# A recurrent attention with a token and channel mixer: the same operations in another issue order and other buffers

## The chip, the cores and the metric

The kernel runs on one core of one Trainium2 chip. The metric is the time of one execution on the device in microseconds (us); less is better. The core has a matrix engine (TensorE, PE in the profile, with PEld for its weight loads), three engines that work through elements (VectorE or DVE, ScalarE or ACT, GpSimd or POOL), SyncE (SP), which here only issues transfers, and 16 DMA engines that carry them.

## The reference

Four batches, eight heads, 768 steps, 48 values a head. A gated linear attention runs along the steps with a state of 48 x 48 a head; its output, heads side by side, is the input of a mixer over tokens and then over channels.

```python
for t in range(S):
    state = alpha[:, :, t, :, None] * state + np.einsum('bhd,bhe->bhde', k[:, :, t], v[:, :, t])
    y[:, :, t] = np.einsum('bhd,bhde->bhe', q[:, :, t], state)
...
xt = x.transpose(0, 2, 1)
h = np.maximum(xt @ w_tok1, 0.0) @ w_tok2
u = x + h.transpose(0, 2, 1)
h2 = np.maximum(u @ w_ch1, 0.0) @ w_ch2
return (u + h2).astype(np.float32)
```

## The kernel before

**Attention** is computed in 12 blocks n = 0 to 11, three to a batch, 256 steps each. Four loads bring alpha, k, q and v of a block (`ld_at`, `ld_kt`, `ld_qt`, `ld_vt`, 384 KB each). ACT takes the logarithm of alpha (`ln`; from block 3 on first the product of two neighbouring steps, `P`, on DVE or POOL, then `lnP`), PE sums it along the steps (`cum`), ACT takes the exponential of the sum and of its negative (`E`, `IE`), and DVE or POOL scales q and k with them (`qq`, `kk`). k and q are then turned: in blocks 0 to 5 by PE (`trk`, `trq`) with a copy out of PSUM (`evk`, `evq`), in blocks 6 to 11 by a DMA transpose (`dk`, `dq`, with a copy `pq`). PE multiplies the two (`G0`, `G1`, one for each half of the block), DVE masks the product (`mask0`, `mask1`), and PE multiplies it with v (`y0`, `y1`) on top of what the state gives (`ia`, `ib`). v is cast and shifted between halves (`vb`, `vs0`, `vs1`), k likewise (`ka`, `kb`, `kc`); `K` is the block's share of the state, `sa` adds the state so far and `sm` scales the sum. `x0`, `x1` take the result out of PSUM.

**The mixer** runs once a batch b: `t1_b_m_kc` multiplies the six pieces of x with the first token weights, `ht` is the ReLU, `t2_b_i` the second token matmul, `u_b_i` adds x. u is turned by PE (`up`, `ut`, batch 0) or a DMA transpose (`ux_b_half`, batches 1 to 3). `c1_b_mc_half` is the first channel matmul in 24 pieces of three instructions, `rt` its ReLU, `c2_b_i_q` the second in quarters of three instructions, `o_b_i` adds u and `st_b_i` stores the tile. The last tile of the last batch is cut into two halves of 192 columns (`h0`, `h1`). Weights are loaded in pieces of 384 KB (`ldw_wt..`, `ldw_wc..`) and cast (`cw_..`) on ACT, DVE or POOL.

**The order is written out as a list.** `build` lists all operations with what each needs; `ORDER` is one list of all their names, and the last letter of each says the engine: t for PE, s for ACT, v for DVE, g for POOL, y for SyncE. The kernel emits them in that order, so on each engine they run in the order in which they stand in the list, and an operation that waits holds all behind it on its engine. `BUFS` gives the number of the buffer for each value in the order in which the values first appear. A value that takes a number used before waits until the readers of the earlier one are done. The pools matter for this: 19 input buffers of 384 KB for all loads (class `in`), 20 buffers for `rt`, 3 for `o`, and eight PSUM banks, in which every PE result lies (class `one` takes one, `pair` two).

**Fillers.** Names such as `f8_trk0` are matmuls on zeros that write nothing that is used. The number counts units of 512 columns; three units are done as one float32 matmul, which the profile shows as two records, the rest as bfloat16 matmuls:

```python
for _ in range(count // 3):
    ...
    self.mm(self.bank(bank)[0:64, 0:384], w, m, True, True)
for _ in range(count % 3):
    ...
    self.mm(self.bank(bank), z, m, True, True)
```

In the profile most attention matmuls and the fillers stand at line 643, the turning by PE at 712, t1 at 878, t2 at 883, c1 at 902, c2 at 907; loads at 584, weight loads at 600 to 607, stores at 624, DMA transposes at 725 and 729. Copies and casts are at 745 (ACT) and 746 (DVE, POOL), the masks at 770, `u` at 887, `o` at 911, `rt` and `ht` at 873 (ACT) and 875 (DVE).

Of the kernel before, what the change touches and what calls it, by code (L numbers as in the profile page):

```python
# [424 lines left out]
ld_kt4y qq4g s0_3v ln15s G1_3t sa1_3v c1_0_2_1t rt_0_2_1s mask0_3v lnP5s c1_0_1_0t c1_0_5_1t rt_0_5_1s rt_0_1_0s r15s
mask1_3v ldw_wc21y cw_wc21s k0a4g ldw_wc20y c1_0_6_1t rt_0_6_1v c1_0_4_0t kk4v ldw_wc22y c1_0_5_0t c1_0_0_0t cw_wc22s
rt_0_4_0v rt_0_0_0v cw_wc20g rt_0_4_1s c1_0_6_0t rt_0_6_0v c1_0_3_1t trq4t rt_0_3_1v cum5t trk4t ld_kt5y k0a5g
ldw_wc23y rt_0_5_0s c2_0_3_0t c2_0_5_0t evq4s kb4s evk4v ld_qt5y G1_4t mask1_4v G0_4t ld_vt4y c2_0_0_0t IE5s c2_0_0_1t
ka4g cw_wc23s c2_0_3_1t kc4s sm1_3g E5s mask0_4v ib3t y1_3t ldw_wc24y cw_wc24s c2_0_5_1t vb4g vs1_4s x1_3s ia4t
ldw_wc25y vs0_4g cw_wc25s ld_at6y y0_3t kk5v c2_0_3_2t y0_4t q0r5v trk5t evk5s qq5v K4t c2_0_0_2t sa0_4v c2_0_0_3t P6v  # L430
x0_3s ld_at7y sm0_4g o_0_0v trq5t x0_4s sa1_4v P7g evq5s lnP6s c2_0_5_2t c2_0_5_3t ld_vt5y vb5g c2_0_4_0t c2_0_4_1t
ld_kt7y kc5g G1_5t G0_5t lnP7s o_0_5v ib4t y1_4t vs1_5s mask1_5v t1_1_1_0t t1_1_1_1t sm1_4g x1_4s c2_0_4_2t c2_0_3_3t
vs0_5s ld_at8y t1_1_1_2t st_0_5s K5t mask0_5v sa0_5v sm0_5v cum6t t1_1_0_0t ld_kt6y k0a6g t1_1_0_1t ld_qt6y c2_0_2_0t
ln17s ld_qt7y ia5t y0_5t x0_5s IE6s kk6g ib5t y1_5t ln16s E6s t1_1_0_2t x1_5v t1_1_0_3t t1_1_1_3t cum7t E7s o_0_3v
# [531 lines left out]
```

## Time and profile before

| What | Value |
|---|---|
| Runs of the kernel | 161.95, 162.28, 163.87 us; median 162.28 |
| Span of the profiled execution, first to last instruction | 160.5 us |
| PE busy | 154.6 us, 96% of the span, 1563 matmul records |
| DVE, ACT, POOL busy | 114.9, 97.8, 80.8 us (72, 61, 50%) |
| Moved by DMA | 35.05 MB, mean 218 GB/s |
| Instructions | 3971 |

For the profiled execution only the span is on record. Times below are counted from the span's start. A row of the timeline gives start, length, engine, line, operation, what is written and read, the shapes, and in brackets how long the engine was idle before and what ended that. A row of the groups gives the number of instructions, their busy time, the mean duration of one in ns, and the idle time ahead of them. A row of stretches gives busy time and number of instructions of each engine, the granted PE clock, the share of the DMA engines and GB/s.

### The profile page before, as it was taken

The numbers are of one execution on the slowest core, as the hardware profiler recorded it, in microseconds if no ns is written. First come the engines' busy times: TensorE is split into PE (matmuls) and PEld (weight loads), VectorE is DVE, ScalarE is ACT, GpSimd is POOL, SyncE is SP. The second block draws the span as 40 slices with busy tenths as digits, with TensorE's granted clock in tenths as the row PEclk, the third lists the DMA queues.
The fourth block names the chain that finished last, engine by engine and source line by source line (L and its number), as shares of the span: only waits on it lengthen the run. The fifth ranks groups of instructions, "written<-read, shape, count | busy, mean of one in ns | idle before, by whom it ended". The sixth has DMA issues, their size and how long they took to land.

```text
span 160.5 us, 3971 instructions
## 1 busy us (share of the span) xinstructions
PE 154.6 (96%) x1563; PEld 97.1 (60%) x1563; DVE 114.9 (72%) x206; ACT 97.8 (61%) x179; POOL 80.8 (50%) x94
## 2 busy tenths in 40 slices
...
DMA packets 76130, 35.05 MB, mean 218 GB/s; under 512 B 70352, under 2 KB 74320, under 8 KB 76112
## 3 DMA queue, kind: packets, MB, share of 16 engines
q1 hardware_dynamic: 73808, 31.76, 74.1%
...
q8 instruction: 12, 0.20, 0.5%
...
HBM read 25.17 MB, written 4.72 MB: 186 GB/s over the span
## 4 chain that ended last, share of the span: by engine, by line
PE 61%; DMA 12%; DVE 6%; ACT 6%; SPq 6%; POOL 4%; issue 3%; DVEq 0%; POOLq 0%
PE ps L907 22%; PE ps L902 21%; PE ps L643 11%; DMA in<-in_v_dram 6%; SPq L584 6%; DMA out_dram<-o 4%; PE ps L878 3%; PE ps L883 2%; DMA ut<-u 2%; DVE pkk L700 2%; DVE gtm L770 1%; PE ps L712 1%; DVE rt L875 1%; POOL vb L746 1%; POOL pkq L700 1%
## 5 line engine op out<-in xcount | busy, mean ns | idle before, releaser
L907 PE MATMUL ps<-wc,rt 128*128 128x384 bf16 (+1 forms) x300 | 52.4, 319 | 0.0
L902 PE MATMUL ps<-ut,wc 128*128 128x384 bf16 x288 | 50.3, 326 | 0.1
L902 PEld LDWEIGHTS <-wc 128*128 128x128 bf16 x288 | 27.1, 98 | 17.9 <-DMA ut<-u 0.6
L907 PEld LDWEIGHTS <-rt 128*128 128x128 bf16 x300 | 27.8, 98 | 16.0
L873 ACT ACTIVATE rt<-ps 128x384 bf16<-128x384 f32 x47 | 21.4, 492 | 23.6 <-PE ps L902 23.3
L875 DVE TENSOR_SCALAR rt<-ps 128x384 bf16<-128x384 f32 x49 | 25.6, 551 | 9.1 <-PE ps L902 8.9
L770 DVE TENSOR_TENSOR gtm<-ps,mk 128x1024 bf16<-128x1024 f32 x24 | 28.5, 1218 | 3.1 <-PE ps L643 2.8
L911 DVE TENSOR_TENSOR o<-ps,u 128x384 f32<-128x384 f32 (+1 forms) x25 | 13.2, 536 | 12.6 <-PE ps L907 10.1
L700 POOL TENSOR_TENSOR pkk<-in,IE 128x768 bf16<-128x768 f32 x8 | 14.5, 1817 | 3.3 <-DVE ss L844 2.3
L745 ACT CAST x<-ps 128x384 bf16<-128x384 f32 x20 | 9.2, 479 | 11.1 <-PE ps L643 9.5
L887 DVE TENSOR_TENSOR u<-ps,x 128x384 bf16<-128x384 f32 x24 | 12.0, 550 | 3.1 <-PE ps L883 2.5
L746 POOL CAST vb<-in 64x384 bf16<-64x384 f32 (+1 forms) x14 | 8.3, 594 | 10.4 <-DMA in<-in_v_dram 4.7
L692 POOL TENSOR_TENSOR in<-in,in 128x384 f32<-128x384 f32 x8 | 8.0, 1000 | 10.5 <-DVE u L887 3.8
L643 PE MATMUL ps<-rt 128*128 128x512 bf16 (+1 forms) x29 | 12.1, 515 | 1.1 <-DVE rt L541 1.1
L745 ACT CAST vb<-in 64x384 bf16<-64x384 f32 (+1 forms) x18 | 11.4, 634 | 0.8 <-DMA in<-in_v_dram 0.3
L700 POOL TENSOR_TENSOR pkq<-in,E 128x768 bf16<-128x768 f32 x6 | 10.9, 1818 | 0.6 <-DMA tpk<-pkq 0.3
L878 PE MATMUL ps<-x,wt 128*128 128x384 bf16 x48 | 11.0, 325 | 0.0
L844 POOL TENSOR_TENSOR ss<-tmp,E 128x384 bf16<-128x384 f32 x10 | 8.3, 833 | 4.2 <-DVE in L628 3.9
L841 DVE TENSOR_TENSOR tmp<-ps,ss 128x384 f32<-128x384 f32 x16 | 8.8, 552 | 1.8 <-PE ps L643 0.6
L883 PE MATMUL ps<-ht,wt 128*128 128x384 bf16 x48 | 9.1, 326 | 0.0
L643 PE MATMUL ps<-vb,gtm 128*128 128x48 bf16 x192 | 8.2, 183 | 0.2 <-DVE gtm L770 0.2
L643 PE MATMUL ps<-tpq,tpk 48*64 48x128 bf16 (+1 forms) x288 | 7.9, 218 | 0.4 <-POOL tpq L746 0.3
...
## 6 DMA issues: line engine op xcount, KB each, us to landing
in<-in_alpha_dram SPq DMA_DIRECT2D x12, 384.0 KB, 5.1
in<-in_v_dram SPq DMA_DIRECT2D x12, 384.0 KB, 5.6
in<-in_k_dram SPq DMA_DIRECT2D x12, 384.0 KB, 5.2
in<-in_q_dram SPq DMA_DIRECT2D x12, 384.0 KB, 5.5
in<-in_moe_w_ch_dram SPq DMA_DIRECT2D x12, 384.0 KB, 5.9
...
in<-in_moe_w_tok_dram SPq DMA_DIRECT2D x4, 384.0 KB, 6.0
...
```

The source lines that it names most:

```text
L643: return self.pe.matmul(out, lhsT=lhsT, rhs=rhs, start=start, stop=stop, skip_group_check=True)
L700: self.shared(self.eng[e].tensor_tensor(self.t(dst)[:, :, h0:h1, 0:D], self.t(src)[:, h0:h1].rearrange("p h s d -> p s h d"), bass.AP(tens ...
L745: return self.act.copy(d, s)
L770: self.nc.vector.tensor_tensor(self.t(gtm)[:, hf, :, :], self.pair(gp).rearrange("p a (j t) -> p (a j) t", t=128), bass.AP(tensor=m.tensor ...
L873: self.act.activation(d, s, AF.Relu)
L875: self.nc.vector.tensor_scalar_max(d, s, 0.0)
L878: self.pe.matmul(self.bank(bank)[:, 0:HD], lhsT=self.wt1[:, kc, m * 128 : m * 128 + 128], rhs=self.t(x), start=(kc == 0), stop=(kc == NS - 1))
L883: self.pe.matmul(self.bank(bank)[:, 0:HD], lhsT=self.wt2[:, kc, i * 128 : i * 128 + 128], rhs=self.t(hts[kc]), start=(kc == 0), stop=(kc = ...
L887: self.nc.vector.tensor_tensor(self.t(u)[:, i % 3], self.bank(bank)[:, 0:HD], self.t(x), ALU.add)
L902: self.pe.matmul(self.bank(bank)[:, 0:HD], lhsT=self.wc1[:, kc, mc * 128 : mc * 128 + 128], rhs=self.t(ut)[:, 3 * half : 3 * half + 3, kc, ...
L907: self.pe.matmul(self.bank(bank)[:, 0 : cz - ca], lhsT=self.t(rts[mc][0])[:, i * 128 : i * 128 + 128], rhs=self.wc2[:, mc, ca:cz], start=( ...
L911: self.nc.vector.tensor_tensor(self.t(o)[:, ca:cz], self.bank(bank)[:, 0 : cz - ca], self.t(u)[:, i % 3, ca:cz], ALU.add)
```

## The change

`ORDER` and `BUFS` are replaced by others; nothing else is touched. The change describes itself as issue order and buffer numbers searched from the present ones with instruction fetches counted on one DMA engine, every operation left as it was. Between the two lists only fillers differ in kind and number (13 entries with 36 units before, 9 with 25 after). Of the other operations some move to another engine: on POOL 79 entries in place of 82, on DVE 186 for 183, on ACT 192 for 194, on SyncE 93 for 91 (two more stores go out from there). The diff, cut to the start and the end of the order and the first line of the buffers:

```diff
-ld_at1y ld_at0y ln1s ln0s f8_cumw1t f1_cumw1t cumw1t IE1s cumw0t IE0s ld_vt0y E0s vb0g vs0_0g vs1_0v ld_kt0y kk0v
-f8_trk0t f1_trk0t trk0t E1s ld_qt0y qq0v ka0s kb0s kc0v f1_trq0t trq0t ld_kt1y kk1v K0t evq0s s0_0v ld_vt1y vb1s
-f1_trk1t trk1t ld_at2y evk0v ln2s f2_G0_0t G0_0t ld_qt1y ka1g sa1_0v f4_cumw2t cumw2t mask0_0v vs0_1s kb1g kc1g vs1_1s
-K1t sm1_0g qq1v sa0_1v sm0_1v G1_0t ld_kt2y IE2s E2s trq1t evq1s ib0t mask1_0v f3_y1_0t y1_0t y0_0t evk1v G0_1t sa1_1v
-ld_qt2y x1_0s mask0_1v G1_1t ld_vt2y x0_0s vb2s kk2g trk2t kc2s ldw_wt10y qq2g cw_wt10s f2_ia1t ia1t mask1_1v evk2s
-trq2t ld_at3y vs1_2g ldw_wt11y evq2v ib1t y1_1t y0_1t vs0_2g ldw_wt21y sm1_1g P3g K2t sa0_2v sm0_2g x0_1s t1_0_0_0t
-f1_G0_2t G0_2t ldw_wt20y G1_2t cw_wt20g t1_0_1_0t mask0_2v x1_1s t1_0_1_1t ld_at4y ld_kt3y t1_0_1_2t lnP3s cum3t
-cw_wt11s IE3s ia2t y0_2t x0_2s t1_0_0_1t t1_0_0_2t E3s t1_0_0_3t mask1_2v t1_0_1_3t ib2t y1_2t ldw_wc14y t1_0_1_4t
-x1_2s t1_0_0_4t f1_t1_0_1_5t t1_0_1_5t ht_0_1v P4g cw_wt21s t1_0_0_5t ht_0_0s f3_t2_0_0t t2_0_0t t2_0_1t u_0_0v ln13s
-r13s ldw_wc13y t2_0_2t u_0_1v t2_0_3t u_0_2v t2_0_5t lnP4s t2_0_4t u_0_3v u_0_5v u_0_4v up_0_0t cw_wc14s cw_wc13s
-ldw_wc15y up_0_1t ld_qt3y k0a3g kk3g cum4t trk3t cw_wc15g ut_0_0v up_0_2t ut_0_2v ut_0_1s c1_0_11_0t c1_0_8_0t IE4s
...
-c2_3_0h1_0t st_3_2s c2_3_0h1_1t c2_3_3_1t c2_3_0h1_2t c2_3_0h1_3t o_3_0h1v st_3_0h1s o_3_5v c2_3_1_0t st_3_5s
-c2_3_3_2t c2_3_3_3t c2_3_4_0t o_3_3v st_3_3y c2_3_4_1t c2_3_4_2t c2_3_4_3t o_3_4v c2_3_1_1t c2_3_1_2t c2_3_1_3t o_3_1v
-st_3_4s c2_3_0h0_0t c2_3_0h0_1t c2_3_0h0_2t c2_3_0h0_3t o_3_0h0v st_3_0h0y st_3_1s
+ld_vt0y ld_at0y vb0g vs0_0g ld_at1y ln0s f12_cumw0t f2_cumw0t cumw0t ln1s ld_kt0y cumw1t IE0s kk0v f2_trk0t trk0t
+ld_qt0y ld_kt1y E0s qq0v ka0v kb0v kc0g trq0t evk0v E1s IE1s kk1v vs1_0s f2_K0t K0t s0_0v ld_at2y sa1_0v ln2s evq0s
+f2_trk1t trk1t evk1v ka1g kc1s ld_vt1y vb1g ld_qt1y qq1v vs1_1s f2_cumw2t cumw2t IE2s vs0_1g sm1_0g G1_0t mask1_0v
+G0_0t ld_kt2y mask0_0v trq1t kk2g kb1s ib0t y1_0t K1t sa0_1v sm0_1g evq1s G1_1t mask1_1v x1_0s E2s ld_vt2y vb2s vs0_2s
+ld_qt2y qq2v sa1_1v f1_trk2t trk2t kc2g G0_1t mask0_1v ia1t ib1t f1_trq2t trq2t evk2s y0_0t K2t y1_1t sm1_1g sa0_2v
+y0_1t x0_1v evq2s G0_2t mask0_2v ldw_wt10y G1_2t ia2t x0_0s cw_wt10s t1_0_0_0t t1_0_1_0t t1_0_1_1t t1_0_1_2t ldw_wt21y
+ld_at4y P4g t1_0_0_1t cw_wt21g sm0_2g f1_ib2t ib2t y0_2t ldw_wt11y cw_wt11s x1_1s t1_0_1_3t mask1_2v vs1_2s y1_2t
+ld_at3y t1_0_0_2t x0_2v t1_0_0_3t t1_0_0_4t P3v ln14s x1_2s t1_0_1_4t t1_0_1_5t ht_0_1v t1_0_0_5t lnP3s cum3t
+ldw_wt20y cw_wt20g ht_0_0s t2_0_2t u_0_2v t2_0_3t u_0_3v lnP4s E3s IE3s ld_kt3y k0a3g ldw_wc13y cw_wc13s ln13s t2_0_1t
+kk3g t2_0_0t u_0_0v t2_0_4t up_0_1t ut_0_1s t2_0_5t u_0_1v ldw_wc14y ldw_wc15y cw_wc15s cum4t up_0_0t trk3t u_0_4v
+u_0_5v up_0_2t ut_0_2s cw_wc14g ut_0_0v c1_0_11_0t ka3v kc3g kb3g r13s E4s c1_0_6_0t rt_0_6_0s c1_0_10_0t IE4s
+c1_0_6_1t rt_0_6_1s ld_qt3y q0r3g qq3g c1_0_7_1t ld_vt3y evk3v c1_0_9_1t rt_0_9_1v ldw_wc10y rt_0_7_1v rt_0_11_0s
+ldw_wc12y cw_wc12s ldw_wc11y cw_wc11g cw_wc10s c1_0_11_1t rt_0_11_1v c1_0_8_0t c1_0_8_1t rt_0_8_1v c1_0_10_1t
+rt_0_10_1v r14s c1_0_9_0t rt_0_9_0s rt_0_8_0s vb3g trq3t evq3v c1_0_7_0t ld_qt4y q0r4g c1_0_0_1t rt_0_0_1v c1_0_2_0t
...
+c2_2_1_2t c2_2_1_3t c2_2_4_0t c2_2_5_0t vs0_11s sm1_10v K11t sa0_11v sm0_11v ib10t y1_10t x1_10s c1_2_9_1t rt_2_9_1v
+c2_2_5_1t ia11t y0_11t ib11t y1_11t t1_3_0_0t t1_3_0_1t t1_3_0_2t t1_3_0_3t x0_11s o_2_1v x1_11v t1_3_1_1t t1_3_0_4t
+t1_3_0_5t t1_3_1_2t t1_3_1_3t t1_3_1_4t t1_3_1_5t ht_3_1v c2_2_5_2t c2_2_5_3t ht_3_0s o_2_5v t2_3_3t st_2_5s t2_3_4t
+u_3_4v t2_3_1t u_3_3v t2_3_5t u_3_5v ux_3_1y u_3_1v t2_3_0t u_3_0v c2_2_4_1t t2_3_2t c2_2_4_2t c2_2_4_3t o_2_4v u_3_2v
+ux_3_0y c2_2_3_0t c2_2_3_1t c2_2_3_2t c2_2_3_3t c1_3_10_1t rt_3_10_1s o_2_3v st_2_3y c1_3_4_1t c1_3_11_1t c1_3_3_1t
+rt_3_3_1v c1_3_2_1t rt_3_2_1v c1_3_1_1t rt_3_4_1v c1_3_0_0t rt_3_0_0s st_2_4s c1_3_8_0t c1_3_2_0t c1_3_3_0t c1_3_1_0t
+rt_3_2_0v rt_3_11_1v rt_3_3_0s c1_3_5_0t rt_3_5_0v c1_3_7_0t rt_3_7_0s c1_3_10_0t c1_3_5_1t c1_3_0_1t rt_3_1_0v
+rt_3_5_1v rt_3_8_0v rt_3_10_0s c1_3_4_0t rt_3_4_0v c1_3_6_0t c2_3_0h1_0t c2_3_1_0t rt_3_0_1s c2_3_0h1_1t c1_3_6_1t
+rt_3_6_1s rt_3_1_1v c1_3_9_0t rt_3_9_0v c2_3_1_1t c1_3_11_0t c2_3_2_0t rt_3_6_0v c2_3_1_2t rt_3_11_0v c2_3_0h0_0t
+c2_3_1_3t o_3_1v c2_3_0h0_1t c1_3_7_1t rt_3_7_1s c2_3_0h1_2t c2_3_0h1_3t o_3_0h1v st_3_0h1y st_2_1s c2_3_5_0t
+c2_3_5_1t c1_3_8_1t c2_3_4_0t rt_3_8_1s c1_3_9_1t rt_3_9_1v st_3_1s c2_3_2_1t c2_3_2_2t c2_3_2_3t o_3_2v c2_3_5_2t
+c2_3_5_3t o_3_5v c2_3_3_0t c2_3_3_1t c2_3_3_2t st_3_2y st_3_5y c2_3_4_1t c2_3_3_3t o_3_3v st_3_3y c2_3_4_2t c2_3_4_3t
+o_3_4v st_3_4y c2_3_0h0_2t c2_3_0h0_3t o_3_0h0v st_3_0h0s
 """
 BUFS = """
-11 8 0 1 0 0 2 1 2 1 0 12 0 0 0 4 2 1 1 0 4 3 8 1 4 0 0 5 1 6 6 9 0 1 7 0 12 0 0 7 2 0 1 0 0 1 0 1 2 4 1 7 1 3 2 2 1 6
...
+0 8 0 1 0 7 0 0 0 1 2 2 1 1 0 7 4 3 4 0 0 5 0 1 7 6 0 1 0 0 0 4 1 1 0 5 1 6 1 4 5 2 0 1 3 0 1 7 7 2 0 3 1 2 1 1 1 3 9
...
```

More of the change, by code (lines that the diff above doesn't have):

```diff
@@ L425 @@
[L425 to L434, printed above, removed]
@@ new lines @@
+rt_0_4_0s ln15s rt_0_4_1s cum5t x0_3s r15s IE5s c1_0_1_1t rt_0_1_1s s0_3v sa1_3v trq4t evq4s c1_0_2_1t rt_0_2_1v G1_3t
+kk4g kb4s E5s c1_0_5_0t mask1_3v trk4t ib3t evk4v ldw_wc21y cw_wc21g c2_0_0_0t ld_qt5y ldw_wc23y y1_3t x1_3v ldw_wc22y
+c1_0_3_0t rt_0_5_0s rt_0_3_0v G0_4t G1_4t mask1_4v mask0_4v cw_wc23s cw_wc22s ldw_wc24y ldw_wc25y cw_wc25s ld_vt4y
+vb4s vs1_4s ka4g q0r5g kc4g c2_0_4_0t cw_wc24g qq5g c2_0_3_0t c2_0_5_0t c2_0_5_1t c2_0_5_2t c2_0_5_3t c2_0_0_1t trq5t
+sm1_3v ld_kt5y k0a5v kk5v ld_vt5y vs0_4s K4t sa0_4v evq5s vb5s c2_0_0_2t c2_0_0_3t trk5t evk5s o_0_5v o_0_0v c2_0_3_1t
@@ new lines @@
+sm0_4g sa1_4v c2_0_3_2t c2_0_3_3t G0_5t o_0_3v G1_5t ia4t y0_4t c2_0_4_1t mask0_5v ld_at6y P6g ld_at7y kc5s sm1_4g
+vs0_5s K5t sa0_5v ln17s P7g c2_0_4_2t x0_4s lnP6s t1_1_0_0t t1_1_0_1t t1_1_1_0t ia5t ib4t vs1_5s y0_5t t1_1_0_2t y1_4t
+ld_at8y sm0_5g ib5t mask1_5v y1_5t cum6t P8v t1_1_1_1t t1_1_1_2t ld_qt7y ld_kt6y k0a6g st_0_3s lnP7s x0_5s x1_5v x1_4s
+t1_1_0_3t t1_1_1_3t t1_1_0_4t ln16s lnP8s IE6s kk6g t1_1_0_5t ht_1_0v t1_1_1_4t t1_1_1_5t ht_1_1s c2_0_4_3t o_0_4v
+cum8t t2_1_1t u_1_1v t2_1_2t u_1_2v t2_1_0t E8s u_1_0v E6s t2_1_3t u_1_3v st_0_5s ld_kt8y ld_qt6y r16s c2_0_1_0t q0r6g
@@ new lines @@
+c2_0_1_1t t2_1_4t c2_0_1_2t qq6v ld_vt6y vb6g t2_1_5t u_1_4v u_1_5v cum7t IE7s vs0_6g k0a8g ln18s c2_0_1_3t o_0_1v
+st_0_1s ka6s vs1_6s r18s ld_kt7y c2_0_2_0t r17s c2_0_2_1t c2_0_2_2t ux_1_0y c1_1_4_0t c1_1_5_0t c1_1_1_0t c1_1_2_0t
+rt_1_1_0s k0a7v kk7v rt_1_2_0s rt_1_5_0s c1_1_0_0t c1_1_6_0t E7s q0r7g qq7g c2_0_2_3t o_0_2v c1_1_7_0t rt_1_0_0v dq6y
+IE8s pq6s rt_1_4_0v kk8v ux_1_1y c1_1_9_1t c1_1_11_1t st_0_0s rt_1_11_1s kb6v c1_1_2_1t c1_1_11_0t c1_1_4_1t rt_1_4_1v
+rt_1_6_0s rt_1_2_1s dk6y c1_1_5_1t rt_1_5_1v c1_1_1_1t c1_1_10_0t ld_qt8y q0r8g kc6s ld_at9y P9v qq8g rt_1_11_0s
@@ new lines @@
+rt_1_9_1s c1_1_6_1t K6t rt_1_1_1s rt_1_10_0v rt_1_6_1s ln19s s0_6v sa1_6v c1_1_10_1t rt_1_10_1s lnP9s c1_1_8_0t
+c1_1_7_1t rt_1_7_1s ld_vt7y ld_at11y vb7g vs1_7g dq7y sm1_6g pq7g c1_1_0_1t rt_1_0_1s rt_1_7_0v vs0_7s G1_6t G0_6t
+c1_1_9_0t rt_1_9_0s kb7s rt_1_8_0v c1_1_8_1t rt_1_8_1s mask1_6v c2_1_2_0t mask0_6v c1_1_3_0t rt_1_3_0v dk7y ka7s
+c1_1_3_1t rt_1_3_1s kc7g y0_6t x0_6v G0_7t mask0_7v G1_7t c2_1_2_1t ib6t y1_6t K7t c2_1_2_2t sa0_7v c2_1_2_3t
+c2_1_3_0t ld_vt8y c2_1_3_1t c2_1_3_2t sm0_7g mask1_7v sa1_7v sm1_7g dq8y pq8s x1_6s dk8y G0_8t o_1_2v G1_8t kc8s cum9t
@@ new lines @@
+E9s vb8g vs0_8s mask1_8v c2_1_1_0t c2_1_1_1t c2_1_1_2t c2_1_1_3t IE9s t1_2_0_0t mask0_8v K8t sa0_8v ia8t y0_8t
+t1_2_0_1t ia7t y0_7t ib7t y1_7t x1_7v c2_1_5_0t r19s x0_7s c2_1_5_1t sm0_8g ib8t t1_2_1_0t vs1_8g t1_2_1_1t t1_2_1_2t
+st_0_4y t1_2_0_2t y1_8t x1_8s x0_8v ld_vt10y ld_kt10y ld_vt9y t1_2_1_3t ld_at10y P10v o_1_1v k0a10v ld_kt9y k0a9g
+lnP10s st_1_2s st_1_1s kk9g c2_1_4_0t t1_2_0_3t t1_2_1_4t ld_qt9y t1_2_1_5t ht_2_1v t1_2_0_4t st_0_2s t1_2_0_5t
+ht_2_0s c2_1_5_2t c2_1_5_3t ld_qt10y ld_kt11y ld_qt11y q0r9g kb9g P11g ln110s r110s t2_2_4t u_2_4v t2_2_3t u_2_3v
```

54 lines of the change are left out of this document (13 added, 41 removed), and 20 rows, old and new, of the table BUFS.

## The prediction

> **What bounds the kernel now.** I read the span and its stretches first, then the waits of the matrix engine, then the timeline of the start and the end.
>
> ```profile
> core 0: us, PE busy (x) PEld busy (x) DVE busy (x) ACT busy (x) POOL busy (x), PEclk, DMA share, GB/s
> 0.00:7.30 7.30, 6.16 (x35) 2.57 (x35) 2.64 (x23) 3.78 (x4) 2.44 (x13) 1.00 0.77 212
> 7.30:31.76 24.46, 23.29 (x288) 14.05 (x285) 20.66 (x29) 22.61 (x36) 15.97 (x18) 1.00 1.10 329
> 31.76:157.42 125.66, 125.19 (x1246) 80.44 (x1246) 91.20 (x153) 71.46 (x140) 62.38 (x64) 1.00 0.76 200
> 157.42:160.50 3.08, 0.00 (x0) 0.00 (x0) 0.36 (x1) 0.00 (x0) 0.00 (x0) 1.00 0.27 96
> ```
>
> The cuts are mine. 31.76 is where the first channel matmul (c1_0_11_0) starts, 157.42 where the last matmul ends. Between them PE is busy 125.19 of 125.66 us: only 0.47 us of idle in 78% of the span. Both orders put the same matmuls behind c1_0_11_0: all filler matmuls lie ahead of it, and the real ones ahead of it are the same set (the first three attention blocks, cum3, cum4, trk3, t1_0, t2_0, up_0). So a new order can win at most 0.47 us in that stretch; it can lose any amount. What is left to win lies in the 31.76 us ahead of it.
>
> There PE looks busy too, but much of that is filler, which computes nothing:
>
> ```profile
> L643 PE MATMUL ps<-rt 128*64 128x384 f32 x14 | 6.9, 607 | 1.1 <-DVE rt L541 1.1
> L643 PE MATMUL ps<-rt 128*128 128x512 bf16 x15 | 5.4, 429 | 0.0
> ```
>
> What ends the waits there is data and the in-order queues of DVE, ACT and POOL: in the second stretch ACT is busy 22.61 of 24.46 us, and DMA stands at a share of 1.10. The chain into c1_0_11_0 reads off the timeline:
>
> ```profile
> 25.99 0.48 ACT L745 CAST x<-ps 128x384 bf16<-128x384 f32 x1
> 27.10 0.49 ACT L873 ACTIVATE ht<-ps 128x384 bf16<-128x384 f32 x1
> 27.73 2.28 PE L883 MATMUL ps<-ht,wt 128*128 128x384 bf16 x12
> 30.16 0.88 POOL L746 CAST wc<-in 128x768 bf16<-128x768 f32 x1 [0.36 <-DMA in<-in_moe_w_ch_dram]
> 31.06 0.55 DVE L746 COPY ut<-ps 128x768 bf16<-128x768 bf16 x1
> 31.76 0.48 PE L902 MATMUL ps<-ut,wc 128*128 128x384 bf16 x2
> ```
>
> The last attention output x1_2 at 25.99, ht at 27.10, the t2 matmuls, then ut and the cast of the 22nd load (wc15), and c1 starts.
>
> **The change, part by part.** No operation but fillers is added or removed; 938 entries become 934.
>
> *Fillers: 36 units of 512 columns become 25* (a float32 matmul is two records and three units: 14 and 15 records become 8 and 13). By the mean durations that is 6 x 0.607 + 2 x 0.429 = 4.5 us less. I cost it at 0: PE waits at those places for DVE, ACT or DMA and would stand idle instead. If a filler were what holds PE, up to 4.5 us would come free, but the floor below cuts that.
>
> *The floor.* c1_0_11_0 needs wc15, the 22nd load in both orders, and its cast.
>
> ```profile
> L605 SPq DMA_DIRECT2D in<-in_moe_w_ch_dram x1: 1363/1363/1363, 25.1 to 25.1; - x1
> DMA to landing us min/median/max: 5.0/5.0/5.0
> L745 ACT CAST wc<-in 128x768 bf16<-128x768 f32 x9 | 7.5, 857 | 0.1
> ```
>
> It is issued at 25.1, lands at 30.1, and a cast takes 0.86: c1 cannot start before 31.0 while loads run at this rate. The head can win 0.75 us at most.
>
> *The head under the new queues.* These rows price the steps:
>
> ```profile
> L770 DVE TENSOR_TENSOR gtm<-ps,mk 128x1024 bf16<-128x1024 f32 x24 | 28.5, 1218 | 3.1 <-PE ps L643 2.8
> L745 ACT COPY tpq<-ps 128x1024 bf16<-128x1024 bf16 x5 | 6.6, 1320 | 0.5 <-PE ps L712 0.5
> L700 DVE TENSOR_TENSOR pkq<-in,E 128x768 bf16<-128x768 f32 x6 | 5.7, 955 | 0.3 <-POOL in L628 0.2
> L746 DVE COPY tpq<-ps 128x1024 bf16<-128x1024 bf16 x1 | 1.3, 1305 | 0.0
> L628 POOL TENSOR_TENSOR in<-in 128x384 f32<-128x384 f32 x8 | 8.0, 999 | 0.4 <-DMA in<-in_alpha_dram 0.3
> L844 POOL TENSOR_TENSOR ss<-tmp,E 128x384 bf16<-128x384 f32 x10 | 8.3, 833 | 4.2 <-DVE in L628 3.9
> L841 DVE TENSOR_TENSOR tmp<-ps,ss 128x384 f32<-128x384 f32 x16 | 8.8, 552 | 1.8 <-PE ps L643 0.6
> ```
>
> DVE's run from kk0 to the last mask of block 2 is dense now. The new order takes evq2 (1.31), kc0 and vs1_0 (half-height copies, an estimate of 0.3 each from the 0.55 of ut above) and sm0_1 (0.55) out of it and puts in qq2 (0.96), ka0 and kb0 (0.3 each) and x0_1 (0.55): 2.5 out, 2.1 in. The first load is now vt0, so at0 lands second and ln1 stands ahead of IE0 on ACT; kk0 starts about where it does now. So mask1_2 ends 0.2 to 0.4 earlier, near 25.2. But it is no longer last. sm0_2 on POOL stands behind P4 and a weight cast: P4 cannot start before at4 lands, the 15th load, some 22.6 (the 17th lands at 24.7, rows below); then 1.0 + 0.86 + 0.83 = 25.3. ib2 and y0_2 follow at 25.9; x0_2 and P3, both now on DVE, end near 27.0; lnP3 on ACT stands ahead of ht_0_0, which starts at 27.5 (27.10 now). Then ACT alone sets the pace:
>
> ```profile
> 28.47 0.51 ACT L634 ACTIVATE la<-in 128x384 bf16<-128x384 f32 x1
> 28.88 1.67 ACT L745 CAST wc<-in 128x768 bf16<-128x768 f32 x2
> L700 POOL TENSOR_TENSOR pkk<-in,IE 128x768 bf16<-128x768 f32 x8 | 14.5, 1817 | 3.3 <-DVE ss L844 2.3 <-PE ps L643 0.7
> L745 ACT COPY ut<-ps 128x768 bf16<-128x768 bf16 x1 | 0.8, 798 | 0.2 <-PE ps L894 0.2
> ```
>
> ht_0_0, lnP4, E3, IE3, cast wc13, ln13, ut_0_1, cast wc15. Five short ones at 0.42 from start to start (28.47 to 28.88), casts and ut at 0.8 (two casts in 1.67): 27.5 + 5 x 0.42 + 3 x 0.8 = 32.0. Beside it kk3 on POOL waits for IE3 (29.2) and with the cast of wc14 ends at 29.2 + 1.82 + 0.86 = 31.9. c1_0_11_0 at 32.0: **+0.25 us**. Bounds: the floor, -0.75; and the slip of the second rival, +3.7.
>
> *The long stretch.* The tightest place that I found is its first microseconds: rt_0_11_0 on ACT stands behind ut_0_2, r13, E4, rt_0_6_0, IE4 and rt_0_6_1. With it that is 0.8 + 6 x 0.45 = 3.5 behind cast wc15, so 35.5; c1_0_8_0, seven c1 steps of 0.49 behind c1_0_11_0, wants its bank at 35.4. Elsewhere the new order gives room: attention blocks 6 and 9 come 5 us of matmul later, block 11 about 2 us. The waits for POOL tpq and DMA ut that make up most of today's 0.47 get cover.
>
> ```profile
> 116.29 0.64 PE L643 MATMUL ps<-tpq,tpk 48*64 48x128 bf16 x32 [0.28 <-POOL tpq L746]
> PEld L902 <- DMA ut<-u: 0.6, 2, 0.5
> ```
>
> The narrow spot at the end is ux_3_1: 4.06 us of matmul between the last t2 that it needs and its first use. Three u on DVE, each 0.55 as the L841 row, end about 1.0 behind that t2, and a transpose takes 3.0 from issue to landing by the row below: 4.0. Loss and gain roughly cancel: **+0.2 us**, bounds -0.47 and +2.
>
> ```profile
> ut<-u SPq DMA_TRANSPOSE x6, 3.0
> ```
>
> *The tail.* Now o of 192 columns runs 0.36 behind the last matmul, and its store, alone, goes out at 157.83. In the new order the store of a full tile (st_3_4) is issued 0.35 before it, and o_3_0h0 queues behind o_3_4 on DVE: **+0.1 us**, bounds 0 and +0.3.
>
> ```profile
> 157.44 0.36 DVE L911 TENSOR_TENSOR o<-ps,u 128x192 f32<-128x192 f32 x1 [0.43 <-PE ps L907]
> 157.83 0.33 SPq L624 DMA_DIRECT2D out_dram<-o  x1
> ```
>
> *Instruction fetches.* The change counts them, so what do they cost? Packets of 16 KB on a queue of their own:
>
> ```profile
> q8 instruction: 12, 0.20, 0.5%
> in<-in_k_dram SPq DMA_DIRECT2D x1, 384.0 KB, 4.8
> in<-in_q_dram SPq DMA_DIRECT2D x1, 384.0 KB, 6.2
> ```
>
> The k load issued at 10.57 lands before the fetch that starts at 15.6 and takes 4.8 us; the q load issued at 11.88 lands after it and takes 6.2. So a fetch costs the loads near it about 1.4 us. Sixteen matmul and weight-load records fewer of 3971 leave about as many fetches, and PE has 0.47 us of idle in all behind 31.76, so I count 0. [...]
>
> **Sum.** 160.5 + 0.25 + 0.2 + 0.1 = 161.05 for the profiled execution. The median of the runs, 162.28, stands 1.78 above its span, so **162.8 us**.
>
> **The rivals.**
>
> *Floor reached.* The sm0_2 detour does not bind, c1 starts at 31.0 and today's idle goes: 162.28 - 0.75 - 0.47 = 161.1. For it: DVE has 0.4 us less work, eleven fillers go. Against it: ACT, nearly full in this stretch, has more ahead of c1, not less.
>
> *Slower: SyncE held at ld_at3.* The new buffer numbers let ld_at3, the 17th load, take the buffer of qt2, so it waits for qq2 on DVE, and SyncE issues nothing behind it. qt2 is the 12th load; the 11th lands at 11.88 + 6.2 = 18.1 by the row above, the next 1.2 later (384 KB at 329 GB/s), and qq2 takes 0.96: 20.3.
>
> ```profile
> 18.90 0.43 SPq L602 DMA_DIRECT2D in<-in_moe_w_tok_dram  x1
> in<-in_moe_w_tok_dram SPq DMA_DIRECT2D x1, 384.0 KB, 5.8
> in<-in_alpha_dram SPq DMA_DIRECT2D x1, 384.0 KB, 3.4
> ```
>
> Today's 17th load goes out at 18.90 and lands at 24.7; the first load of all, with nothing ahead of it, took 3.4. So it decides when qq2 ends after 24.7 - 3.4 = 21.3: from there each microsecond shifts loads 17 to 22 and c1. qq2 needs E2, which stands on ACT behind evq1 and x1_0, and mask1_1 ahead of it on DVE. Were qq2 done only at 25.0, c1 would slip 3.7: 166.0. Against it: my walk leaves 1.0 us.
>
> *Small stalls add up.* Four or five places like rt_0_11_0 at 0.3 to 0.5 each: 162.28 + 1.7 = 164.0. For it: eight PSUM banks, and, counted through the order, some seventeen places where a bank or an input comes back within 1.0 us of matmul. Against it: the present order has as many and loses 0.47.
>
> *Cold clock.* The first filler records, nine units in 4.2 us, run at 0.46 us a unit; two units later on take 0.59 together, drain included.
>
> ```profile
> 1.06 4.21 PE L643 MATMUL ps<-rt 128*64 128x384 f32 x7 [1.06 <-DVE rt L541]
> 19.53 0.59 PE L643 MATMUL ps<-rt 128*128 128x512 bf16 x2
> ```
>
> So PE starts at about half rate, though the clock column says 1.00. If fewer fillers let it fall back once, another 4.2 us at half rate cost 2.1: 164.9. [...]
>
> **How the numbers follow.** Forecast 0.52, floor reached 0.22, stalls add up 0.12, SyncE held 0.12, cold clock 0.02. A change of 2% is 3.25 us, about what a measurement of this kernel can tell from no change. Faster than 159.0 is under the floor, left at 0.02 in case loads land earlier. Slower than 165.5 takes most of SyncE held and a little of the two before and after it: 0.13. Within: 0.85. The range goes from the floor, 161.0, to 165.4, just short of SyncE held.
>
> **What would show it.** Right: c1 (L902) starts between 31.5 and 32.5, behind a cast of wc on ACT; the stretch from there to the last matmul is 125.3 to 126.3 long; no wait of PE for DMA tpk; the end lies 3.0 to 3.3 behind the last matmul. Wrong: a first L902 ahead of 31.0 or behind 33.5, a gap in the landings near 24, or idle of PE over 1.5 us behind c1.

## The result and the profile after

The changed kernel took **164.39 us** (median, 162.78 to 166.74) and the kernel before 162.5 us beside it (20 executions each): a ratio of **1.0085, 95% interval 1.0058 to 1.0113**. All ratios here leave out the slow executions, those over 1.5% above the fastest of their kernel: four of these 20 (165.31 to 166.74), and three of the ten (164.15 to 164.56) of the kernel with four output buffers below. The change makes the kernel slower by 0.9%, or 1.4 us, less than the 2% that the forecast took as about what can be told from no change, but clear in this many runs. The two profiled executions differ by more, 162.6 against 160.5 us, so 2.1 us have to be found in them.

The stretches of the changed kernel, cut like those of before at the first c1 and at the last matmul (7.30 is kept as it was), with the same columns:

```profile
0.00:7.30 7.30, 6.25 (x24) 2.55 (x25) 2.64 (x23) 2.68 (x3) 3.38 (x14) 1.00 0.81 216
7.30:31.91 24.61, 20.66 (x289) 13.81 (x287) 21.26 (x31) 22.80 (x35) 14.12 (x16) 1.00 1.09 325
31.91:159.24 127.33, 125.18 (x1249) 80.31 (x1246) 92.44 (x154) 71.14 (x143) 61.37 (x61) 1.00 0.77 196
159.24:162.60 3.36, 0.00 (x1) 0.00 (x0) 0.40 (x2) 0.00 (x0) 0.00 (x0) 0.97 0.40 146
```

c1 starts at 31.91 in place of 31.76 (+0.15), the tail is 3.36 in place of 3.08 (+0.28), and the long stretch is 127.33 in place of 125.66 (+1.67). PE does the same work in it, 125.18 us; its idle time grew from 0.47 to 2.15. That idle lies in three places. These are all the waits of PE behind the first c1 in the changed kernel, by what ended them (engine, line, releaser: us in total, times, longest):

```profile
PE ps L883 <- DVE o L911: 1.2, 1, 1.2
PE ps L902 <- DMA ut<-u: 0.6, 1, 0.6
PE ps L643 <- POOL tpq L746: 0.3, 1, 0.3
```

**The largest, at 100.05.** One t2 matmul (t2_2_1) waits for an `o`, and the `o` for a DMA. The timelines of PE, DVE, ACT and SP around it:

```profile
98.16 0.65 PE L907 MATMUL ps<-wc,rt 128*128 128x384 bf16 x3
100.05 0.48 PE L883 MATMUL ps<-ht,wt 128*128 128x384 bf16 x2 [1.24 <-DVE o L911]
...
99.44 0.56 DVE L911 TENSOR_TENSOR o<-ps,u 128x384 f32<-128x384 f32 x1 [1.87 <-DMA out_dram<-o]
99.91 1.01 DVE L887 TENSOR_TENSOR u<-ps,x 128x384 bf16<-128x384 f32 x2
...
93.86 0.93 ACTq L624 DMA_DIRECT2D out_dram<-o  x2
...
83.46 0.45 SPq L584 DMA_DIRECT2D in<-in_v_dram  x1
...
93.25 1.16 SPq L584 DMA_DIRECT2D in<-in_q_dram  x1
DMA to landing us min/median/max: 1.6/2.1/6.8
```

t2_2_1 needs the PSUM bank that o_1_5 reads. o_1_5 shares one of the three output buffers with o_1_1, and must wait until st_1_1 has carried o_1_1 out. That store is issued at 93.86, in a run of nine loads of 384 KB which SyncE issued from 83.46 to 94.41 and of which four are still on the way, and lands only at 99.35. The last line is that of all stores, from issue to landing: 2.1 us at the median, 6.8 at the most. Counted from issue to issue of the matmuls, PE loses 1.40 us.

The store stands on ACT's queue, not on that of the loads, and is late all the same: 5.48 us from issue to landing. DMA engines that are simply full would fit this (from 90 to 101 us their share is 1.12); what holds the store inside them no run here shows. An instruction fetch of 0.95 us that starts at 94.96 may have a part in it.

The same wait stood in the kernel before. The waits of DVE for stores, before and then after:

```profile
DVE o L911 <- DMA out_dram<-o: 2.5, 3, 1.6
DVE o L911 <- DMA out_dram<-o: 2.1, 2, 1.9
```

DVE waited longer for stores before than after. But there all six `u` of that batch were done by 98.74, and o_1_3, which waited for a store, came at 99.19, o_1_5 at 107.53. In the new order o_1_5 stands ahead of u_2_2 on DVE and of t2_2_1 on PE, and the same kind of wait reaches the engine that bounds the kernel.

**The second, at 68.04**, 0.80 us: c1_1_4_0 waits for the transpose ux_1_0. **The third, at 82.38**, 0.44 us: G0_7 waits for the copy of a transposed q (pq7) on POOL. Timeline rows of SP and PE:

```profile
63.63 1.58 SPq L729 DMA_TRANSPOSE ut<-u  x1
68.04 0.99 PE L902 MATMUL ps<-ut,wc 128*128 128x384 bf16 x5 [0.63 <-DMA ut<-u]
...
80.99 1.33 POOL L746 COPY tpq<-tpk 128x1024 bf16<-128x1024 bf16 x1 [0.32 <-DMA tpk<-pkq]
82.38 0.64 PE L643 MATMUL ps<-tpq,tpk 48*64 48x128 bf16 x32 [0.28 <-POOL tpq L746]
```

ux_1_0 is issued at 63.63 with loads still under way (ld_kt7 lands at 66.23) and lands 4.36 us later; before it took 2.89 and its first use came 1.7 us later.

**The head** ended as walked. From the timeline of the start:

```profile
20.27 0.37 SPq L584 DMA_DIRECT2D in<-in_alpha_dram  x1
27.05 0.47 ACT L873 ACTIVATE ht<-ps 128x384 bf16<-128x384 f32 x1
28.16 1.00 POOL L692 TENSOR_TENSOR in<-in,in 128x384 f32<-128x384 f32 x1 [0.69 <-DMA in<-in_k_dram]
31.00 0.91 ACT L745 CAST wc<-in 128x768 bf16<-128x768 f32 x1
31.91 0.81 PE L902 MATMUL ps<-ut,wc 128*128 128x384 bf16 x4
```

ld_at3 goes out at 20.27, released by qq2, ht_0_0 starts at 27.05, and the cast of wc15 ends where c1 begins. **The tail:** the last `o` queues behind o_3_4 on DVE and its store goes out 0.43 behind the last matmul.

```profile
158.78 0.85 DVE L911 TENSOR_TENSOR o<-ps,u 128x384 f32<-128x384 f32 x2 [0.32 <-PE ps L907]
159.67 0.34 ACTq L624 DMA_DIRECT2D out_dram<-o  x1
```

### The profile page after: what moved, and what is told of

Read it like the earlier page. It is cut to its first block, busy times and chain, and to the rows that moved or that the text cites. A ratio compares the mean times of both kernels' runs of the same rounds, so it can differ in the third digit from the quotient of the medians.

```text
span 162.6 us, 3966 instructions
## 1 busy us (share of the span) xinstructions
PE 152.1 (94%) x1555; PEld 96.7 (59%) x1555; DVE 116.7 (72%) x209; ACT 96.6 (59%) x179; POOL 78.9 (49%) x91
## 4 chain that ended last, share of the span: by engine, by line
PE 58%; DMA 25%; SPq 6%; POOL 3%; DVE 3%; issue 2%; ACT 1%; ACTq 0%; DVEq 0%; POOLq 0%
PE ps L907 24%; PE ps L902 22%; DMA in<-in_q_dram 11%; PE ps L643 7%; DMA in<-in_k_dram 4%; SPq L584 4%; DMA tpk<-pkq 4%; DMA out_dram<-o 3%; DMA in<-in_alpha_dram 3%; PE ps L878 2%; PE ps L712 2%; PE ps L883 1%; DVE o L911 1%; POOL pkk L700 1%; POOL in L696 1%
## 5 line engine op out<-in xcount | busy, mean ns | idle before, releaser
L873 ACT ACTIVATE rt<-ps 128x384 bf16<-128x384 f32 x50 | 23.4, 491 | 23.7 <-PE ps L902 23.2
L875 DVE TENSOR_SCALAR rt<-ps 128x384 bf16<-128x384 f32 x46 | 23.7, 552 | 11.1 <-PE ps L902 10.7
L844 POOL TENSOR_TENSOR ss<-tmp,E 128x384 bf16<-128x384 f32 x12 | 10.0, 836 | 11.5 <-DVE tmp L841 11.3
L700 POOL TENSOR_TENSOR pkq<-in,E 128x768 bf16<-128x768 f32 x7 | 12.7, 1820 | 1.1 <-DVE in L628 0.8
L745 ACT CAST x<-ps 128x384 bf16<-128x384 f32 x16 | 7.5, 476 | 8.8 <-PE ps L643 8.6
L700 POOL TENSOR_TENSOR pkk<-in,IE 128x768 bf16<-128x768 f32 x6 | 10.9, 1816 | 1.7 <-DVE in L692 1.4
L696 POOL TENSOR_TENSOR in<-in,lf 128x384 f32<-128x384 f32 x9 | 9.0, 1001 | 4.8 <-ACT rt L873 1.8
L746 POOL CAST vb<-in 128x768 bf16<-128x768 f32 (+1 forms) x13 | 8.8, 679 | 4.0 <-DVE pkq L700 2.2
L643 PE MATMUL ps<-rt 128*128 128x512 bf16 (+1 forms) x21 | 9.0, 536 | 1.1 <-DVE rt L541 1.1
L700 DVE TENSOR_TENSOR pkk<-in,IE 128x768 bf16<-128x768 f32 x6 | 5.7, 956 | 4.8 <-ACT IE L687 4.3
```

The costliest lines, as they stand in the source:

```text
L643: return self.pe.matmul(out, lhsT=lhsT, rhs=rhs, start=start, stop=stop, skip_group_check=True)
L700: self.shared(self.eng[e].tensor_tensor(self.t(dst)[:, :, h0:h1, 0:D], self.t(src)[:, h0:h1].rearrange("p h s d -> p s h d"), bass.AP(tens ...
L745: return self.act.copy(d, s)
L873: self.act.activation(d, s, AF.Relu)
L875: self.nc.vector.tensor_scalar_max(d, s, 0.0)
```

## The experiments

Theory: the 1.67 us are single waits of PE, the largest because an output buffer comes back late. Rivals: the loads are at fault whatever the buffers; a wait that is removed comes back at the next late place; the missing fillers cost something. All runs start from the changed kernel unless said, and ratios are to the kernel before. "Idle" is that of PE between the first c1 and the last matmul, from the row of that stretch. Span, c1 and idle are those of the one execution that was profiled. "No fillers" and "SyncE held" rest on two executions each, "ux_1_0 ahead of a load" on four.

| Kernel | Ratio, 95% interval | Span | c1 starts | Idle |
|---|---|---|---|---|
| before | 1 | 160.5 | 31.76 | 0.47 |
| after | 1.0085 [1.0058, 1.0113] | 162.6 | 31.91 | 2.15 |
| four output buffers | 1.0006 [0.997, 1.0043] | 161.7 | 31.87 | 1.16 |
| o_1_5 in another buffer | 1.0027 [0.9978, 1.0075] | 162.1 | 31.27 | 1.99 |
| two loads later | 1.0075 [1.0041, 1.0109] | 163.3 | 31.54 | 2.85 |
| ux_1_0 ahead of a load | 1.0145 [1.0101, 1.019] | 163.7 | 31.61 | 3.24 |
| all three places moved | 1.0126 [1.0084, 1.0169] | 162.8 | 31.52 | 2.16 |
| two fillers left | 1.0079 [1.0038, 1.0121] | 162.7 | 31.26 | 2.51 |
| no fillers | 1.0171 [1.0065, 1.0277] | 163.9 | 32.44 | 2.43 |
| SyncE held | 1.0376 [1.0272, 1.048] | 167.1 | 36.46 | 2.06 |
| four buffers, two moves | 1.0009 [0.9979, 1.0039] | 160.9 | 31.69 | 0.66 |

### Four output buffers

```diff
-"rt": 20, "o": 3
+"rt": 19, "o": 4
# o_1_5: buffer 2 -> 3, o_1_3: 0 -> 2; rt_1_9_1: 19 -> 2, rt_3_5_0: 19 -> 16
```

> The changed kernel with a fourth output buffer: o_1_5 takes number 3 and o_1_3 takes number 2; to make room the two rt values of buffer 19 move to buffers 2 and 16, free at that time. Order untouched. Theory (store): PE's stall of 1.40 us ahead of t2_2_1 comes from o_1_5 on VectorE, which waits until the store of o_1_1 has landed (99.35), because that store was issued at 93.9 in the middle of nine loads. Then o_1_5 runs at 97.6, right behind u_2_5, the stall falls under 0.2 us and the span from 162.6 to 161.2 to 161.4; against the kernel before the ratio is about 1.00. Rival (order): VectorE would come to u_2_2 late anyway; the stall stays over 1 us and so does the span. Rival (given back): the stall goes but ux_2_0 then ends a wait of the same size at the first c1_2 of half 0; the span stays at 162.4 or more.

Measured: 1.0006. The order is untouched, only buffer numbers differ, and the wait at t2_2_1 is gone (DVE, then PE, then the long stretch):

```profile
97.97 0.55 DVE L911 TENSOR_TENSOR o<-ps,u 128x384 f32<-128x384 f32 x1
99.13 0.49 PE L883 MATMUL ps<-ht,wt 128*128 128x384 bf16 x2
31.87:158.37 126.50, 125.34 (x1247) 80.28 (x1246) 92.51 (x154) 71.36 (x143) 61.28 (x61) 1.00 0.77 199
```

From 1.0085 to 1.0006 is 1.3 us of 162.5, and the wait taken away was 1.40. The waits for ux_1_0 (0.93) and at block 7 (0.30) are still there, another one of 0.42 has come at G0_5, and yet the ratio to the kernel before is 1 within its interval.

### o_1_5 in another of the three buffers

```diff
# o_1_5: buffer 2 -> 1, o_1_4: 1 -> 2
```

> The changed kernel with o_1_5 in output buffer 1 in place of 2 (and o_1_4, the next to use 1, in 2). Buffer 1 is that of o_1_2, whose store landed at 98.45, 0.90 us ahead of the store of o_1_1 at 99.35. Theory (store): o_1_5 starts 0.9 us sooner, so the stall ahead of t2_2_1 falls from 1.40 to about 0.5 us, and the span from 162.6 to about 161.7; three buffers, same order, same loads. Rival (it is the number of buffers or the rt values moved in the run with four): stall stays near 1.4.

```profile
97.38 0.56 DVE L911 TENSOR_TENSOR o<-ps,u 128x384 f32<-128x384 f32 x1 [0.91 <-DMA out_dram<-o]
97.99 0.48 PE L883 MATMUL ps<-ht,wt 128*128 128x384 bf16 x2 [0.29 <-DVE o L911]
...
116.58 1.23 SPq L725 DMA_TRANSPOSE tpk<-pkk  x1
119.35 0.64 PE L643 MATMUL ps<-tpq,tpk 48*64 48x128 bf16 x32 [1.35 <-DMA tpk<-pkk]
```

Now o_1_5 waits for st_1_2, which lands at 97.35, and starts at 97.38: the store of that buffer sets its date. The wait at t2_2_1 is 0.45 us. So 1.40, 0.45 and 0 us of this wait stand against 1.0085, 1.0027 and 1.0006; the last two differ by less than their intervals. In the profiled execution something else shows as well: G1_11 at 119.35 now waits 1.51 us for the transpose of kk11, which is issued at 116.58.

### Two loads later

```diff
-ld_qt10y ld_kt11y ld_qt11y q0r9g
+ld_qt10y q0r9g
...
-ux_2_1y c2_1_4_3t
+ux_2_1y ld_kt11y ld_qt11y c2_1_4_3t
```

> The changed kernel with ld_kt11 and ld_qt11 moved behind ux_2_1 on SyncE, so that seven loads stand around the three stores in place of nine; buffers and all else untouched. Theory (store): the stores of o_1_2, o_1_1 and o_0_2 land some 2.4 us sooner (96 to 98.5 in place of 98.5 to 101.1), o_1_5 runs at about 97.6 with the same three buffers, the stall of 1.40 us falls under 0.3 and the span to 161.2 to 161.5. Rival (buffers alone): the stores land as late as now and nothing changes. Rival (order): stall over 1 us.

```profile
DMA to landing us min/median/max: 1.6/2.0/4.5
98.14 0.55 DVE L911 TENSOR_TENSOR o<-ps,u 128x384 f32<-128x384 f32 x1
93.72 1.90 ACTq L624 DMA_DIRECT2D out_dram<-o  x2
96.21 1.14 PE L883 MATMUL ps<-ht,wt 128*128 128x384 bf16 x6 [0.63 <-ACT ht L873]
117.86 1.23 SPq L725 DMA_TRANSPOSE tpk<-pkk  x1
120.63 0.58 PE L643 MATMUL ps<-tpq,tpk 48*64 48x128 bf16 x27 [1.07 <-DMA tpk<-pkk]
```

With seven loads in place of nine, two of them still on the way in place of four, the longest store takes 4.5 us in place of 6.8, st_1_1 lands at 97.58 and o_1_5 no longer waits. So the loads make the store late; the instruction fetch, which starts at 94.30 here, is there in both. But nothing is gained by the ratio. In the profile ACT is held by the issue of a store until 95.62 and ht_2_0 comes late (0.79 us at t2_2_4), and G1_11 waits 1.23 us. That execution took 165.03, the longest of those that count, and its G0_7, ahead of the moved loads, already waits 0.98 us in place of 0.44; so not all of its idle comes from the move. In the changed kernel the place at G1_11 had only 0.8 us to spare:

```profile
116.34 1.23 SPq L725 DMA_TRANSPOSE tpk<-pkk  x1
119.90 0.64 PE L643 MATMUL ps<-tpq,tpk 48*64 48x128 bf16 x32
```

The transpose (issued 116.34, landed 119.06) stands at the end of POOL's chain for blocks 9 to 11, of which pq9, q0r11, qq11, vb10, k0a11, pq10 and kk11 follow one another without a gap from the landing of dq9 on, some 10 us, with 2.7 us of transpose behind them. Here dq9 lands at 108.07 in place of 106.36, and the chain ends 1.5 us later.

### ux_1_0 ahead of a load

```diff
-r18s ld_kt7y c2_0_2_0t
+r18s c2_0_2_0t
...
-ux_1_0y c1_1_4_0t
+ux_1_0y ld_kt7y c1_1_4_0t
```

> The changed kernel with ld_kt7 moved behind ux_1_0 on SyncE; all else untouched. Theory: the wait of 0.80 us ahead of c1_1_4_0 comes from ux_1_0 queuing behind three loads on the DMA engines (issued at 63.6, landed at 68.0, 4.4 in place of 3.0 us). With one load fewer ahead it lands near 66.8, the wait falls under 0.2 us, and the span to about 161.9. Rival: the transpose is held by something else, and the wait stays; or the late kt7 holds k0a7 on VectorE and gives the time back behind 69 us.

```profile
63.43 1.34 SPq L729 DMA_TRANSPOSE ut<-u  x1
71.82 4.56 PE L902 MATMUL ps<-ut,wc 128*128 128x384 bf16 x27 [0.72 <-DMA ut<-u]
PE ps L883 <- DVE o L911: 1.6, 1, 1.6
```

ux_1_0 lands at 66.42 and its wait is gone. The load now stands ahead of dq6 and ux_1_1: ux_1_1 lands at 71.78 and c1_1_9_1 waits 0.88 us for it, c1_1_8_0 0.50, G0_8 0.73, and t2_2_1 1.77. A wait of 0.80 was exchanged for four.

### All three places moved

```diff
# the two moves above, and:
-ld_at11y ... dq7y sm1_6g pq7g
+dq7y ld_at11y ... pq7g sm1_6g
```

> The changed kernel with both moves of loads (ld_kt11 and ld_qt11 behind ux_2_1, ld_kt7 behind ux_1_0), dq7 ahead of ld_at11 on SyncE and pq7 ahead of sm1_6 on GpSimd, which is to end the wait of 0.44 us ahead of G0_7. If the three waits are what the changed kernel loses, the span is 162.6 - 1.4 - 0.8 - 0.4 = 160.0 (up to 160.5), and against the kernel before the ratio is 0.995 to 1.000. If they are only where a loss shows that comes from elsewhere (matmul, clock), it stays near 162.

```profile
PE ps L643 <- DMA tpk<-pkk: 1.1, 1, 1.1
```

The waits at c1_1_4_0 and G0_7 are gone, that at t2_2_1 is 0.35; in their place stand 0.72 at c1_1_9_1, 0.47 at c1_1_8_0 and 1.27 at G1_11. The theory that the three waits can simply be added up and taken away fails here: each move of a transfer pushes others.

### Fillers

```diff
# two fillers left:
-f2_trk0t ... f2_K0t ... f2_trk1t ... f2_cumw2t ... f1_trk2t ... f1_trq2t ... f1_ib2t
# no fillers: besides these
-f12_cumw0t f2_cumw0t
```

> The changed kernel without its seven filler entries behind the first two (11 units of 512 columns, no longer done). Forecast's step (fillers cost nothing, they fill waits): the first c1 starts at 31.6 to 32.2 as with them (31.9), the span stays at 162.2 to 163.0. Rival (a filler holds PE): c1 at 31.0 to 31.4. Rival (cold clock): PE falls back to half rate in the start, two 512-column steps no longer pass in 0.6 us, c1 at 33 or later and the span 164 or more.

> The changed kernel without any filler. Now PE is idle until cumw0 at about 6.3. If PE starts at half rate, as the slow first fillers say, cumw0 takes about 2 us in place of 1.05 and the next matmuls likewise until some 4 us of work are done; IE0 and kk0 then start 0.5 to 0.9 us later, and c1 at 32.0 to 33.5 (later, as the chain through VectorE and ScalarE passes the delay on; the floor by the 22nd load is 31.9). If the slow first fillers have another cause, cumw0 keeps its 1.05 us and c1 starts at 31.9.

Without the seven later fillers the time stays: 1.0079. c1 at 31.26 lies in the rival's range and not in that of the forecast's step, but with all fillers it came at 31.27 in another run above, so it decides nothing. Without the two at the start the first real matmuls take 1.12 us for three in place of 0.65 (first row without fillers, second after), c1 starts at 32.44, and the granted clock falls later. The last two rows are the stretches 18 to 20 and 20 to 22 us of that kernel; the clock is the third number from the end (line numbers are one lower in these two kernels):

```profile
6.30 1.12 PE L642 MATMUL ps<-la,u 128*128 128x384 bf16 x3 [6.30 <-ACT la L636]
6.35 0.65 PE L643 MATMUL ps<-la,u 128*128 128x384 bf16 x3
18.00:20.00 2.00, 1.40 (x20) 1.03 (x22) 1.87 (x3) 1.95 (x4) 1.68 (x2) 0.64 1.08 356
20.00:22.00 2.00, 2.00 (x26) 1.80 (x27) 2.00 (x3) 1.18 (x2) 1.12 (x2) 0.50 0.72 240
```

### SyncE held at ld_at3

```diff
# ld_at3: input buffer 10 -> 9 (that of vt2, read last by vs1_2), ldw_wc25 9 -> 10,
# ld_vt4 10 -> 9, ld_at10 9 -> 10, ld_qt9 10 -> 9
```

> The changed kernel with input buffers 9 and 10 exchanged from ld_at3 on: ld_at3 takes the buffer of vt2 and waits for vs1_2 on ScalarE (ends at 25.1) in place of qq2 (20.2); ldw_wc25 takes the other. By the forecast's rival of SyncE held at ld_at3: from 21.1 on (24.5, where load 17 lands, less 3.4) each microsecond shifts loads 17 to 22, so 4.0 us; wc15 lands near 35.0, c1 starts near 35.9, and the span is near 166.6. Rival (the DMA engines catch up, and only P3 and what hangs on it is late): load 17 lands at 28.5, c1 at 33.5 to 34.5, span 164 to 165.

```profile
25.29 0.37 SPq L584 DMA_DIRECT2D in<-in_alpha_dram  x1
35.63 0.90 ACT L745 CAST wc<-in 128x768 bf16<-128x768 f32 x1
36.46 0.81 PE L902 MATMUL ps<-ut,wc 128*128 128x384 bf16 x4
36.46:163.72 127.26, 125.20 (x1249) 80.28 (x1246) 92.52 (x154) 71.16 (x143) 61.30 (x61) 1.00 0.77 197
```

ld_at3 goes out 5.02 us later than in the changed kernel and c1 starts 4.55 later. The long stretch, 127.26 us, is unchanged, so a delay of the head goes into the time whole: the span grows by 4.5 us, and 1.0376 against 1.0085 is 4.7. Expected were c1 near 35.9 and a span near 166.6; 36.46 and 167.1 came.

### Four buffers and two moves on PE

```diff
# o and rt buffers as in the first experiment, and:
-c2_0_2_2t ux_1_0y c1_1_4_0t ... c2_0_2_3t
+c2_0_2_2t c2_0_2_3t ux_1_0y c1_1_4_0t
...
-c2_3_0h0_0t c2_3_1_3t ... c2_3_0h0_1t ... st_3_4y c2_3_0h0_2t
+c2_3_1_3t ... st_3_4y c2_3_0h0_0t c2_3_0h0_1t c2_3_0h0_2t
```

> The changed kernel with four output buffers as before (o_1_5 in the fourth, o_1_3 in the third), and two moves on PE alone: c2_0_2_3 (three matmuls, 0.49 us) ahead of c1_1_4_0, the matmul that waits for ux_1_0, and the first half of c2_3_0h0 (six matmuls, about 0.5 us) behind c2_3_4_3, so that the last full tile is stored earlier. Theory (the excess of the stretch is single waits of PE, each filled by work put in front of it): the wait ahead of c1_1_4_0 falls from 0.93 to about 0.45, the tail from 3.4 to 3.0 to 3.2; span about 161.0, ratio 0.996 to 1.001 to the kernel before. Rival (time won ahead of block 11 is given back at G1_11 or G0_7, whose POOL chains set the date): those waits grow by 0.3 to 0.5, span 161.5 to 162, ratio 1.000 to 1.004.

```profile
31.69:157.73 126.04, 125.38 (x1247) 80.39 (x1246) 92.55 (x154) 71.25 (x143) 61.35 (x61) 1.00 0.77 200
82.02 0.64 PE L643 MATMUL ps<-tpq,tpk 48*64 48x128 bf16 x32 [0.57 <-POOL tpq L746]
```

The wait for ux_1_0 is gone, G0_7 waits 0.73 in place of 0.30, idle is 0.66 and the tail 3.17. Both accounts came true in part. The profiled span is 0.8 us shorter than with four buffers alone, but the execution profiled there took 0.7 us more than the median of those that count, and here 0.2 less. The runs give 1.0009 [0.9979, 1.0039]: against 1.0006 the two moves can't be told from nothing. No version here beats the kernel before.

## Why the prediction was right or wrong

**The sum.** 162.8 us was forecast, and 164.39 came: inside the range, no difference over 2%, but 1.6 us too low. The median stands 1.79 above the profiled span, as assumed (1.78); so the miss lies in the terms.

**The head: right.** +0.25 forecast, +0.15 measured, c1 behind the cast of wc15 on ACT as walked. qq2 ended at 20.24 (forecast 20.3), sm0_2 at 24.94 (25.3), IE3 at 28.71 (29.2). One thing was off: the pace was not ACT's alone; ut_0_1 ahead of the cast of wc15 ended just as wc15 landed (30.98), and the cast started at 31.00, so that an emptier ACT would have won nothing. ht_0_0 also started at 27.05 and not at 27.5, and ACT then stood 0.31 us until wc13 had landed. That two errors cancelled to within 0.1 us is partly luck. Over the runs that keep this head c1 started between 31.27 and 31.91, so single profiles carry some 0.6 us of scatter here, more than the term itself.

**The long stretch: the term that was mis-sized.** +0.2 forecast, +1.67 measured, within its bounds of -0.47 and +2. Here the prediction's own sign of being wrong came: idle of 2.15 us behind c1, over the 1.5 that it named; and 127.33 lies outside its 125.3 to 126.3. The step that failed is "loss and gain roughly cancel". It came from a search for tight places among PSUM banks, ACT and the turned blocks; the three output buffers, and the time that a store takes amid loads, were not looked at, though the line of the stores was at hand. The place named as the tightest, rt_0_11_0, cost PE nothing, and ux_3_1 came in time. "The waits for POOL tpq and DMA ut ... get cover" was wrong for both: 0.3 and 0.6 us are among the three new waits. The room seen at block 11 was no room: the matmuls come later, but its k is turned later too, dk11 landing at 119.06 in place of 112.22. PE did not wait for it in the changed kernel, as forecast ("no wait of PE for DMA tpk"), but 0.8 us less would have been too little, as three experiments show.

**The tail:** +0.28, near its upper bound of 0.3 rather than 0.1, and 3.36 lies outside the 3.0 to 3.3 named. The queue behind o_3_4 is there but costs nothing: the last store goes out 0.43 us behind the last matmul, as before. What grew is the store's landing, 1.84 us in place of 1.61, with st_3_4 issued 0.3 us ahead of it. So the cause given for this term was wrong.

**Fillers at 0: right** for this change, as the ratio of the kernel with two fillers shows. Those at the start may be worth some half a microsecond, by c1 of one profile (32.44 for 31.91), which is no more than c1 scatters; both orders have them.

**Instruction fetches at 0: right as to PE**, twelve of 16 KB as before. But ld_kt3, on its way while the one that starts at 25.22 ran, landed 2.50 us behind the load before it, where 1.0 to 1.2 is usual, and k0a3 waited for it (0.69 us, the row at 28.16 above).

**The rivals.** "Small stalls add up" (0.12, 164.0) came nearest, with three waits of 0.4 to 1.4 us rather than four or five of 0.3 to 0.5; it deserved more than "floor reached" (0.22), which needed all idle to go. "SyncE held" did not happen, since qq2 ended a microsecond ahead of the point from which it decides, but its price is now measured: 4.55 us of c1 for an issue at 25.29, where its rule of 1 us each from 21.3 on gives 4.0. "Cold clock" did not happen: the mean granted clock of the changed kernel's executions is 0.996 to 1.000. Its chance of 0.02 was the author's estimate; in other runs the clock did fall, as told below, but the price of 2.1 us did not show there: of the executions with two fillers that count, those at 0.99 took 163.99 to 164.25 us and the others 163.55 to 164.45.

**What stays open.** The kernel with four buffers measures like the one before while its profile has 0.7 us more idle. The execution that was profiled took 163.44 us, where the median of those that count is 162.75, so that profile shows 0.7 us that most executions don't have. Whether the four buffers win back the whole loss stays open all the same: the interval reaches 1.0043, and the median of all ten executions is 163.15 against 162.44.
